# Weight conversion in PSUM banks, one exponential for two heads, and a 384 + 192 column split of the last attention product

## The chip, the cores and the metric

The kernel runs on one core of one Trainium2 chip. A core has five engines that run side by side, each through its own list of instructions in order: PE (matrix products, with a separate track PEld for loading weights), DVE (vector work), ACT (activation functions and copies), POOL (general work) and SP (which issues the transfers). The metric is device time in microseconds (us) of one execution; lower is better.

## The reference

Eight batches of eight heads go through linear attention with random features, and the result, 4608 tokens of width 512, goes through a two-layer network.

```python
def phi(x):
    proj = np.einsum('bhsd,md->bhsm', x, omega)        # 64 -> 128 features
    h = proj - np.sum(x * x, axis=-1, keepdims=True) / 2.0
    return np.exp(h - np.max(h, axis=-1, keepdims=True)) / np.sqrt(m)
kv = np.einsum('bhsm,bhsd->bhmd', k_p, v)
z = np.sum(k_p, axis=2)
num = np.einsum('bhsm,bhmd->bhsd', q_p, kv)
den = np.einsum('bhsm,bhm->bhs', q_p, z)[..., None] + 1e-06
x = num / den
...
h = x @ w_in                                            # 512 -> 2048
sp = np.maximum(h, 0.0) + np.log1p(np.exp(-np.abs(h)))
out = (h * erf(sp)) @ w_out                             # 2048 -> 512
```

The two weight matrices arrive as 64-bit floats; everything else is 32-bit.

## The kernel before

**Attention.** The work is cut into 32 pairs (batch, two heads), written `b_p` in the names. Sequence length is 576, so a pair has 1152 rows of q and k, the first head's 576 and then the second's. For each pair PE projects k and q into 128 features, three tiles of 384 rows each (`ppk`, `ppq`); DVE takes the maxima (`mxk`, `mxq`), ACT the exponentials (`fk`, `fq`); PE sums keys times values (`kvp`), which DVE or ACT copies to `kh` (with a rest `kl` from pair 8 on); PE turns the query features (`pt`, three tiles of 384), which DVE and ACT copy to `qh` (and a rest `ql`). The last product `nd` multiplies `kh` and `qh`: for each of the two heads it gives 64 rows of numerators and 64 rows of the denominator, repeated; the second head has them the other way up (`rows`). It is made in four tiles of 288 columns, one for each head and half. For the first eight pairs (`WHOLE = 8`) it is one product in 32-bit floats; from then on it is three products in fp32r, PE's faster 32-bit format, on a high part and a rest of each operand. For each tile ACT takes the logarithm of the denominators and then the exponential of its negative (`rc`, 64 rows each), and DVE multiplies numerators by it into `xs`.

**Network.** Each batch goes through two halves (`ph`) of 1024 hidden columns. The first layer gives tiles `h` (for the first three batches), later seven products `hS`, `hA` in place of eight; then softplus, erf and a product (`gs`, `hs`), a high part `gh` and a rest `gl`; the second layer gives tiles `o`. All these products have 288 columns and use three fp32r matmuls: high by high, high by rest, rest by high.

**Weights.** Each of 32 weight blocks is converted once, by `make`, the first time that it is needed (all in the first quarter of the run), and stored; later uses fetch the stored form. A 64-bit block `st` of 128 by 512 lands; `w_bias` scales its upper word into `wt`, `w_shift` shifts it, `w_sign` and `w_tail` (two DVE instructions with two inputs, `st` and `wt`) put in sign and tail, `w_high` rounds to fp32r and `w_rest` takes the difference. `wt` lies in ordinary on-chip memory (pool `gh`), bias and high may be done by POOL or ACT, the rest by DVE or POOL.

**Order.** Nothing is placed by hand. `build` lists all operations with their engines and costs, tiles and due times, and `Plan.order` goes through them as a list scheduler would: each engine, when free, takes the ready operation that is due first, if its tiles have a free slot. The order that comes out is fixed in the program. `SLOTS` gives slots in each pool (8 banks in PSUM, pool `ps`), `CAPS` how many of them one stream may hold at once: `att` attention tiles, `moe1` and `moe2` the network's, and `early(n)` replaces the cap of `att` for the four pairs of the first batch.

Of the kernel before, what the change touches and what calls it, by code (L numbers as in the profile page):

```python
# [319 lines left out]
def build(emit):  # L322
# [36 lines left out]
    def parts(t, src, keys):  # L359

        ks = range(2)
        pl.op("whigh", [("A", 0.63, -1e9), ("G", 0.7, WHG)], lambda e: E.w_high(e, t, src),
              reads=keys, writes=[(t, ("h", k)) for k in ks])
        pl.op("wrest", [("V", 0.68, -1e9), ("G", 1.3, 3.0)], lambda e: E.w_rest(e, t, src),
              reads=keys + [(t, ("h", k)) for k in ks], writes=[(t, ("l", k)) for k in ks])

    def make(u, t):

        nm = "_".join(str(c) for c in u)
        st = pl.tile("gl", f"st{nm}", [P, HW, 2], I32, "st")  # L370
# [12 lines left out]

    def unit(u, block=None):
# [127 lines left out]
    def attend(n, t0):  # L512
        a = pairs[n]
        x = xs[n] = pl.tile("xs", f"xs{a['nm']}", [P, 2, T])
        for j in range(2):
            for t in range(2):
                nd = pl.tile("ps", f"nd{a['nm']}_{j}_{t}", [P, 512], F32, "att", early(n))
                rc = pl.tile("rc", f"rc{a['nm']}_{j}_{t}", [P, T])
                c = range((j * S + t * T) // 384, (j * S + (t + 1) * T - 1) // 384 + 1)
                pl.op("nd", [("T", 0.5 if n < WHOLE else 3 * COST["mm"], -1e9)],  # L520
                      lambda e, j=j, t=t, nd=nd: E.attend(nd, a["kh"], a["kl"], a["qh"], a["ql"], j, t),
                      reads=[(a["kh"], 0), (a["kl"], 0)] + [(a["qh"], i) for i in c]
                      + [(a["ql"], i) for i in c], writes=[(nd, 0)],
                      plan=pair_time(n, t0 + 0.1 * j + 0.05 * t))
# [200 lines left out]
def tile_attention_moe(ctx: ExitStack, tc: tile.TileContext, qT, kT, vP, omT, w1, w2, out):  # L725
# [66 lines left out]
    class Emit:  # L792
# [243 lines left out]
```

## Time and profile before

| what | us |
|---|---|
| median of 3 runs | 1103.33 (1102.34 to 1104.43) |
| span of the profiled execution | 1101.4 |
| median less span | 1.9 |
| PE, DVE, ACT, POOL busy (shares) | 98%, 65%, 64%, 40% |
| transfers | 231 MB, 210 GB/s |

The profiled execution is known by its span, from the first to the last instruction of the program; the median of the runs is 1.9 us above it. Busy time of PE is the union of its matmuls, which overlap one another, so that a busy PE need not be at its peak: where times of single matmuls are needed, the distance from one start to the next is taken.

### The profile page before, as it was taken

Reading aid. Unit: us, or ns where it says so; the run is one execution under the profiler, and the core shown is the slowest. Engines: PE = TensorE matmul, PEld = TensorE weight load, DVE = VectorE, ACT = ScalarE, POOL = GpSimd, SP = SyncE. Lnnn points to the kernel's source line nnn. Section 1 sums busy time; section 2 is a strip of 40 time slices with the busy share of each in tenths; the row PEclk is TensorE's granted clock in tenths of the full one; section 3 lists DMA queues with packets and bytes.
Section 4 is the critical chain, followed back from the end, with each engine's and each line's share of the span. In section 5 each row is a group of like instructions: output and inputs, shape, how many; then the busy total and the mean of one; then the engine's idle time right before and its main releaser. Section 6 shows DMA issues by size and latency. Waiting matters only on the chain.

```text
span 1101.4 us, 21514 instructions
## 1 busy us (share of the span) xinstructions
PE 1074.1 (98%) x8272; PEld 1063.9 (97%) x8272; DVE 715.1 (65%) x1257; ACT 709.0 (64%) x1354; POOL 435.1 (40%) x353
## 2 busy tenths in 40 slices
PE   7798899999999999999999999999999999999998
PEld 6698899999999999999999999999999999999998
DVE  5967789876377575955757566675656766464541
ACT  7777769776578766756647667476566764654440
POOL 6535336210075294822436343343334413252300
PEclk9899899999999999999999999999999999999999
DMA  8546568675557666666666777657765666567771
GB/s 241 174 132 205 173 231 279 198 257 162 171 176 251 205 204 242 190 215 226 216 211 207 225 216 222 211 181 247 232 225 185 214 216 208 193 226 278 254 241 58
DMA packets 70117, 231.27 MB, mean 210 GB/s; under 512 B 8288, under 2 KB 8672, under 8 KB 70016
## 3 DMA queue, kind: packets, MB, share of 16 engines
q1 hardware_dynamic: 69952, 229.84, 63.9%
q8 instruction: 66, 1.08, 0.4%
q14 instruction: 35, 0.29, 0.1%
q0 software_dynamic: 64, 0.07, 0.0%
HBM read 195.26 MB, written 34.60 MB: 209 GB/s over the span
## 4 chain that ended last, share of the span: by engine, by line
PE 91%; DVE 4%; ACT 1%; issue 1%; DMA 1%; SPq 1%; POOL 0%; DVEq 0%
PE o L742 36%; PE h L742 13%; PE hS L742 11%; PE hA L742 8%; PE ppq L742 5%; PE kvp L742 5%; PE ppk L742 5%; PE nd L742 5%; PE pt L742 2%; DVE wt L742 1%; DMA uk<-kT 1%; SPq L742 1%; DVE qh L742 0%; DVE hs L742 0%; DVE mxk L742 0%
## 5 line engine op out<-in xcount | busy, mean ns | idle before, releaser
L742 PE MATMUL o<-gh,w 128*128 128x288 f32 x2048 | 444.8, 298 | 7.8 <-POOL w L742 7.4
L742 PEld LDWEIGHTS o<-gh,w 128*128 128x128 f32 x2048 | 338.9, 188 | 9.0 <-POOL w L742 8.0
L742 PE MATMUL o<-gl,w 128*128 128x288 f32 x1024 | 301.9, 295 | 0.0
L742 PEld LDWEIGHTS o<-gl,w 128*128 128x128 f32 x1024 | 192.7, 188 | 0.2
L742 PE MATMUL h<-xh,w 128*128 128x288 f32 x768 | 178.8, 305 | 0.9 <-ACT hs L742 0.9
L742 PE MATMUL hS<-xh,wS 128*128 128x288 f32 x640 | 165.7, 302 | 1.1 <-issue 1.1
L742 ACT ACTIVATE fk<-ppk,mxk 128x128 f32<-128x128 f32 x288 | 83.3, 371 | 78.0 <-DVE mxk L742 77.6
L742 PEld LDWEIGHTS h<-xh,w 128*128 128x128 f32 x768 | 131.2, 191 | 1.6 <-ACT hs L742 1.3
L742 PE MATMUL hA<-xh,w 128*128 128x288 f32 x480 | 122.1, 299 | 0.0
L742 ACT ACT_TABLE_LOAD x92 | 118.0, 1283 | 2.4 <-PEq L1027 0.7
L742 PEld LDWEIGHTS hS<-xh,wS 128*128 128x128 f32 x640 | 114.8, 189 | 1.3 <-issue 1.3
L742 PE MATMUL h<-xl,w 128*128 128x288 f32 x384 | 113.9, 297 | 0.0
L742 ACT ACTIVATE fq<-ppq,mxq 128x128 f32<-128x128 f32 x288 | 83.2, 371 | 40.0 <-DVE mxq L742 39.5
L742 POOL TENSOR_TENSOR gl<-hs,gh 128x576 fp32r<-128x576 f32 x50 | 86.5, 1753 | 42.2 <-ACT gh L742 25.8
L742 POOL TENSOR_TENSOR uq<-uq 64x576 f32<-64x576 f32 x40 | 46.4, 1178 | 139.6 <-DMA uq<-qT 98.1
L742 POOL TENSOR_TENSOR hs<-gs,hs 128x576 f32<-128x576 f32 x40 | 65.1, 1649 | 85.8 <-ACT gs L742 66.0
L742 DVE TENSOR_REDUCE mxk<-ppk 128x3 f32<-128x384 f32 x96 | 52.8, 556 | 68.9 <-PE ppk L742 67.8
L742 PE MATMUL hS<-xl,wS 128*128 128x288 f32 x320 | 94.5, 295 | 0.0
L742 POOL TENSOR_TENSOR uk<-uk 64x576 f32<-64x576 f32 x44 | 53.5, 1234 | 93.1 <-DMA uk<-kT 91.6
L742 ACT ACTIVATE gh<-hs 128x1152 fp32r<-128x1152 f32 x49 | 56.4, 1164 | 48.1 <-DVE hs L742 19.4
L742 PEld LDWEIGHTS hA<-xh,w 128*128 128x128 f32 x480 | 85.9, 189 | 0.0
L742 PE MATMUL ppk<-wk,uk 128*128 128x128 f32 x576 | 79.2, 279 | 4.4 <-DVE wk L742 4.1
(94 smaller groups left out, 2124.4 us busy)
## 6 DMA issues: line engine op xcount, KB each, us to landing
w<-wdw SPq DMA_DIRECT2D x184, 512.0 KB, 4.3
wS<-wdcS SPq DMA_DIRECT2D x80, 512.0 KB, 4.0
st<-w SPq DMA_DIRECT2D x32, 512.0 KB, 5.2
wdw<-w SPq DMA_DIRECT2D x32, 512.0 KB, 3.9
v<-vP SPq DMA_DIRECT2D x32, 325.0 KB, 3.5
w<-wdw SPq DMA_DIRECT2D x40, 256.0 KB, 3.7
out<-os SPq DMA_DIRECT2D x32, 288.0 KB, 4.0
uk<-kT SPq DMA_DIRECT2D x31, 288.0 KB, 4.2
```

The costliest lines, as they stand in the source:

```text
L742: return tc.keep_in_program_order(method(*args, **kwargs))
```

## The change

- `make` takes `wt` from the PSUM pool `ps` (one bank each, at most two at once, stream `wp`) and no longer from `gh`. POOL doesn't reach PSUM, so bias and high are on ACT alone, shift, sign, tail and rest on DVE alone, under new names (`pbias`, `pshift`, ...) and with new costs. The six instructions themselves stay the same.
- `attend` makes `nd` in tiles of 384 and 192 columns (`SPANS`). The two heads' logarithms of one span go into one `rc` tile of 128 rows, and one exponential covers both. There is one `rc` slot for each span.
- `early` gives the first four pairs up to seven banks, where it was five, and `att` may hold five, where it was four.

```diff
-CAPS = dict(st=2, wt=2, cv=2, att=4, moe1=3, moe2=2)
+CAPS = dict(st=2, wt=2, wp=2, cv=2, att=5, moe1=3, moe2=2)
...
+SPANS = ((0, 384), (384, 192))
...
-        w = pl.tile("gh", f"wt{nm}", [P, HW], I32, "wt")
-        pl.op("wbias", [("G", 0.8, WBG), ("A", 0.67, -1e9)], lambda e: E.w_bias(e, st, w),
+        w = pl.tile("ps", f"wt{nm}", [P, HW], I32, "wp")
+        pl.op("pbias", [("A", 0.67, -1e9)], lambda e: E.w_bias(e, st, w),
...
-        pl.op("wshift", [("V", 0.42, -1e9)], lambda e: E.w_shift(w), reads=[(w, 0)], writes=[(w, 0)])
+        pl.op("pshift", [("V", 0.68, -1e9)], lambda e: E.w_shift(w), reads=[(w, 0)], writes=[(w, 0)])
...
     def early(n):
-        return 5 if n < NP else None
+        return 7 if n < NP else None
...
-            act.activation(rc.ap[num], nd.ap[den, :T], AF.Ln, bias=eps[den])
+            act.activation(rc.ap[num], nd.ap[den, :w], AF.Ln, bias=eps[den])
...
-        def exp_den(self, rc, j):
-            num = rows(j)[0]
-            act.activation(rc.ap[num], rc.ap[num], AF.Exp, scale=-1.0)
+        def exp_den(self, rc):
+            act.activation(rc.ap, rc.ap, AF.Exp, scale=-1.0)
```

The new `attend`, which takes the place of the loop over heads and halves:

```python
for t, (c0, w) in enumerate(SPANS):
    rc = pl.tile(f"rc{t}", f"rc{a['nm']}_{t}", [P, w])
    nds = [pl.tile("ps", f"nd{a['nm']}_{j}_{t}", [P, 512], F32, "att", early(n)) for j in range(2)]
    for j, nd in enumerate(nds):
        pl.op("nd", [("T", (4 if n < WHOLE else 3) * COST["mm"] * w / T, -1e9)], ...)
    for j, nd in enumerate(nds):
        pl.op("ndlog", [("A", 0.25 + 0.00083 * w, -1e9)], ...)
    pl.op("ndexp", [("A", 0.2 + 0.00083 * w, -1e9)], lambda e, rc=rc: E.exp_den(rc), ...)
    for j, nd in enumerate(nds):
        pl.op("divide", [("V", 0.15 + 0.00105 * w, -1e9)], ...)
```

Because the planner sees other costs and slots, the whole order changes. Two places follow. The first is DVE's list in the second pair of the run, `0_1`, up to the two copies that make its `qh` (here `0_1` is the pair, a last number counts tiles, `wt1_0_1` is a weight block of the first layer). Before:

```order
L742 TENSOR_TENSOR w1_0_0_1_147<-wt1_0_0_254,w1_0_0_1_147 128x2x256
L742 TENSOR_REDUCE mxq_0_1_258<-ppq_0_1_2_286 128x3
L742 TENSOR_SCALAR wt1_0_1_269<-wt1_0_1_269 128x512
L742 SCALAR_TENSOR_TENSOR wt1_0_1_269<-st1_0_1_157,wt1_0_1_269 128x512
L742 TENSOR_REDUCE mxk_0_2_335<-ppk_0_2_0_322 128x3
L742 TENSOR_TENSOR xs_0_0_277<-nd_0_0_1_0_245,rc_0_0_1_0_290 64x288
L742 TENSOR_REDUCE mxk_0_2_335<-ppk_0_2_1_331 128x3
L742 TENSOR_REDUCE mxk_0_2_335<-ppk_0_2_2_338 128x3
L742 COPY qh_0_1_360<-pt_0_1_0_350 128x384
L742 TENSOR_TENSOR xs_0_0_277<-nd_0_0_1_1_247,rc_0_0_1_1_293 64x288
L742 SCALAR_TENSOR_TENSOR wt1_0_1_269<-st1_0_1_157,wt1_0_1_269 128x512
L742 COPY qh_0_1_360<-pt_0_1_2_367 128x384
```

Now, the same place up to the same two copies:

```order
L751 TENSOR_SCALAR wt1_0_0_264<-wt1_0_0_264 128x512
L751 SCALAR_TENSOR_TENSOR wt1_0_0_264<-st1_0_0_150,wt1_0_0_264 128x512 x2
L751 COPY kh_0_1_304<-kvp_0_1_278 128x2x64
L751 COPY kh_0_1_304<-kvp_0_1_278 128x128
L751 TENSOR_REDUCE mxk_0_2_314<-ppk_0_2_0_300 128x3
L751 TENSOR_REDUCE mxk_0_2_314<-ppk_0_2_1_310 128x3
L751 TENSOR_TENSOR xs_0_0_330<-nd_0_0_0_0_233,rc_0_0_0_298 64x384
L751 TENSOR_REDUCE mxk_0_2_314<-ppk_0_2_2_317 128x3
L751 TENSOR_TENSOR xs_0_0_330<-nd_0_0_1_0_240,rc_0_0_0_298 64x384
L751 COPY qh_0_1_345<-pt_0_1_0_333 128x384
L751 COPY qh_0_1_345<-pt_0_1_2_349 128x384
```

The second weight block (`wt1_0_1`) and the first block's rest have moved behind these copies, the copy of `kh` has come in from ACT, and the two copies of `qh` stand next to each other.

The second place is the conversion of `w2_0_0_0`, the block that the first second-layer product waits for. Before, POOL does its bias, high and rest, between those of other blocks:

```order
L742 TENSOR_SCALAR wt2_0_0_0_1250<-st2_0_0_0_1174 128x512
L742 TENSOR_TENSOR w1_1_3_12_1125<-wt1_1_3_1186,w1_1_3_12_1125 128x2x256
L742 TENSOR_SCALAR wt2_0_0_1_1268<-st2_0_0_1_1255 128x512
L742 TENSOR_SCALAR w2_0_0_0_13_1175<-wt2_0_0_0_1250 128x2x256
L742 TENSOR_TENSOR w2_0_0_0_13_1175<-wt2_0_0_0_1250,w2_0_0_0_13_1175 128x2x256
```

Now POOL has none of it, and DVE's list reads there:

```order
L751 TENSOR_SCALAR wt2_0_0_0_1320<-wt2_0_0_0_1320 128x512
L751 SCALAR_TENSOR_TENSOR wt2_0_0_0_1320<-st2_0_0_0_1206,wt2_0_0_0_1320 128x512
L751 TENSOR_REDUCE mxk_1_3_1375<-ppk_1_3_0_1331 128x3
L751 TENSOR_REDUCE mxk_1_3_1375<-ppk_1_3_1_1342 128x3
L751 TENSOR_REDUCE mxk_1_3_1375<-ppk_1_3_2_1347 128x3
L751 COPY qh_1_2_1370<-pt_1_2_1_1382 128x384
L751 TENSOR_TENSOR w1_1_3_12_1101<-wt1_1_3_1306,w1_1_3_12_1101 128x2x256
L751 SCALAR_TENSOR_TENSOR wt2_0_0_0_1320<-st2_0_0_0_1206,wt2_0_0_0_1320 128x512
L751 TENSOR_TENSOR xs_1_1_1297<-nd_1_1_1_1_1166,rc_1_1_1_1292 64x192
L751 COPY hs0_1_1_1340<-h010_1_1_1360 128x288
L751 TENSOR_SCALAR wt2_0_0_1_1425<-wt2_0_0_1_1425 128x512
L751 TENSOR_TENSOR w2_0_0_0_13_1207<-wt2_0_0_0_1320,w2_0_0_0_13_1207 128x2x256
```

On PE the first second-layer product moves from row 323 of the list to row 404: it stood in the middle of the products of `w1_1_1`, and now stands behind those of `w1_1_3` and most of pair `1_3`.

More of the change, by code (lines that the diff above doesn't have):

```diff
@@ L357, in store, with parts @@
               plan=clock[0] + 10.0, size=P * HW * 8)
-    def parts(t, src, keys):
+    def parts(t, src, keys, banked=False):
         ks = range(2)
-        pl.op("whigh", [("A", 0.63, -1e9), ("G", 0.7, WHG)], lambda e: E.w_high(e, t, src),
+        pl.op("phigh" if banked else "whigh", [("A", 0.63, -1e9)] + [("G", 0.7, WHG)] * (not banked),
+              lambda e: E.w_high(e, t, src),
               reads=keys, writes=[(t, ("h", k)) for k in ks])
-        pl.op("wrest", [("V", 0.68, -1e9), ("G", 1.3, 3.0)], lambda e: E.w_rest(e, t, src),
+        pl.op("prest" if banked else "wrest", [("V", 0.68, -1e9)] + [("G", 1.3, 3.0)] * (not banked),
+              lambda e: E.w_rest(e, t, src),
               reads=keys + [(t, ("h", k)) for k in ks], writes=[(t, ("l", k)) for k in ks])
@@ L514, in attend @@
         x = xs[n] = pl.tile("xs", f"xs{a['nm']}", [P, 2, T])
[L515 to L521, printed above, removed]
+        for t, (c0, w) in enumerate(SPANS):
+            rc = pl.tile(f"rc{t}", f"rc{a['nm']}_{t}", [P, w])
+            nds = [pl.tile("ps", f"nd{a['nm']}_{j}_{t}", [P, 512], F32, "att", early(n)) for j in range(2)]
+            for j, nd in enumerate(nds):
+                c = range((j * S + c0) // 384, (j * S + c0 + w - 1) // 384 + 1)
+                pl.op("nd", [("T", (4 if n < WHOLE else 3) * COST["mm"] * w / T, -1e9)],
+                      lambda e, j=j, c0=c0, w=w, nd=nd:
+                      E.attend(nd, a["kh"], a["kl"], a["qh"], a["ql"], j, c0, w),
@@ L529, in attend @@
-                pl.op("divide", [("V", 0.47, -1e9)], lambda e, j=j, t=t, nd=nd, rc=rc: E.divide(x, nd, rc, j, t),
-                      reads=[(nd, 0), (rc, 0)], writes=[(x, (j, t))])
+                      plan=pair_time(n, t0 + 0.1 * t + 0.05 * j))
+            for j, nd in enumerate(nds):
+                pl.op("ndlog", [("A", 0.25 + 0.00083 * w, -1e9)],
+                      lambda e, j=j, w=w, nd=nd, rc=rc: E.log_den(rc, nd, j, w),
+                      reads=[(nd, 0)], writes=[(rc, j)], set="exp")
@@ L532, in split @@
+            pl.op("ndexp", [("A", 0.2 + 0.00083 * w, -1e9)], lambda e, rc=rc: E.exp_den(rc),
+                  reads=[(rc, 0), (rc, 1)], writes=[(rc, 0), (rc, 1)], set="exp")
+            for j, nd in enumerate(nds):
+                pl.op("divide", [("V", 0.15 + 0.00105 * w, -1e9)],
+                      lambda e, j=j, c0=c0, w=w, nd=nd, rc=rc: E.divide(x, nd, rc, j, c0, w),
+                      reads=[(nd, 0), (rc, j)], writes=[(x, (j, i)) for i in range(t, 2)])
     def split(b, c):
@@ L904, in turn_rest, with attend, log_den, divide @@
             dve.tensor_sub(ql.ap[:, c], pt.ap[:, :3 * P], qh.ap[:, c].bitcast(F32))
-        def attend(self, nd, kh, kl, qh, ql, j, t):
-            c = slice(j * S + t * T, j * S + (t + 1) * T)
+        def attend(self, nd, kh, kl, qh, ql, j, c0, w):
+            c = slice(j * S + c0, j * S + c0 + w)
             if kh is kl:
-                pe.matmul(nd.ap[:, :T], lhsT=kh.ap[:, j, :], rhs=qh.ap[:, c], start=True, stop=True)
+                pe.matmul(nd.ap[:, :w], lhsT=kh.ap[:, j, :], rhs=qh.ap[:, c], start=True, stop=True)
                 return
             for i, (l, r) in enumerate(((kh, qh), (kh, ql), (kl, qh))):
-                pe.matmul(nd.ap[:, :T], lhsT=l.ap[:, j, :], rhs=r.ap[:, c], start=i == 0, stop=i == 2)
-        def log_den(self, rc, nd, j):
+                pe.matmul(nd.ap[:, :w], lhsT=l.ap[:, j, :], rhs=r.ap[:, c], start=i == 0, stop=i == 2)
+        def log_den(self, rc, nd, j, w):
             num, den = rows(j)
-            act.activation(rc.ap[num], nd.ap[den, :T], AF.Ln, bias=eps[den])
-        def exp_den(self, rc, j):
+            act.activation(rc.ap[num], nd.ap[den, :w], AF.Ln, bias=eps[den])
+        def exp_den(self, rc):
+            act.activation(rc.ap, rc.ap, AF.Exp, scale=-1.0)
+        def divide(self, x, nd, rc, j, c0, w):
             num = rows(j)[0]
-            act.activation(rc.ap[num], rc.ap[num], AF.Exp, scale=-1.0)
-        def divide(self, x, nd, rc, j, t):
-            num = rows(j)[0]
-            dve.tensor_mul(x.ap[num, t, :], nd.ap[num, :T], rc.ap[num])
+            dve.tensor_mul(x.ap.rearrange("p t c -> p (t c)")[num, c0:c0 + w], nd.ap[num, :w], rc.ap[num])
         def x_high(self, e, h, src, i, n):
```

11 lines of the change are left out of this document (3 added, 8 removed).

## Prediction

> **What bounds the kernel now.** I read the page first.
>
> ```profile
> span 1101.4 us, 21514 instructions
> PE 1074.1 (98%) x8272; PEld 1063.9 (97%) x8272; DVE 715.1 (65%) x1257; ACT 709.0 (64%) x1354; POOL 435.1 (40%) x353
> PE   7798899999999999999999999999999999999998
> PEclk9899899999999999999999999999999999999999
> ```
>
> PE is the bound, and it falls short only in the first six slices of 27.5 us. So a step is worth what it takes out of PE's gaps there, or adds to PE's own work anywhere. The windows view sizes the gaps (PE, PEld, DVE, ACT, POOL busy, then PE's granted clock):
>
> ```profile
> 14.50:58.80 44.30, 36.17 (x231) 30.25 (x229) 37.48 (x67) 34.75 (x102) 28.21 (x27) 0.88 0.61 193
> 27.00:35.00 8.00, 5.04 (x14) 3.33 (x14) 7.18 (x11) 4.69 (x14) 6.92 (x7) 0.57 0.33 127
> 35.00:58.80 23.80, 20.64 (x145) 18.28 (x144) 21.94 (x44) 19.03 (x56) 10.61 (x11) 0.93 0.49 167
> 106.00:116.00 10.00, 1.70 (x5) 0.79 (x4) 9.38 (x9) 9.93 (x13) 8.02 (x6) 0.68 0.50 184
> 116.00:140.00 24.00, 23.92 (x173) 23.92 (x174) 17.48 (x25) 17.96 (x32) 7.96 (x8) 0.92 0.50 168
> 116.00:220.00 104.00, 103.74 (x791) 102.67 (x792) 86.61 (x129) 80.97 (x167) 41.30 (x40) 0.98 0.67 220
> 460.00:536.00 76.00, 73.49 (x561) 72.51 (x560) 48.77 (x91) 45.16 (x89) 31.58 (x22) 0.98 0.65 213
> ```
>
> Where PE stalls, DVE is busy 90 to 94% (7.18 of 8.00, 21.94 of 23.80, 9.38 of 10.00): those stretches are DVE's. A stall also costs clock (0.57 and 0.68). The waits of PE, and the chain of work for PE's own pace:
>
> ```profile
> PE o L742 <- POOL w L742: 7.4, 2, 6.9
> PE nd L742 <- DVE qh L742: 6.8, 6, 2.5
> PE ppk L742 <- DVE xs L742: 0.4, 1, 0.4
> 38.58 2.06 PE ppk L742 x18
> 70.98 0.98 PE pt L742 x9
> 72.77 1.94 PE nd L742 x8
> 352.21 1.96 PE kvp L742 x18
> 1059.42 38.13 PE o L742 x288
> ```
>
> A plain 32-bit product is two records. So a projection of a pair (ppk, likewise ppq) takes 2.06 us, kvp 1.96, pt 0.98, a plain nd pair 1.94, and an fp32r matmul of 288 columns 38.13/288 = 132.4 ns.
>
> **Term A, the first four pairs (14.5 to 58.8).** PE has there nd of the first pair, three pairs of 2.06 + 2.06 + 1.96 + 0.98 + 1.94 = 9.0 us, and six fp32r matmuls: 1.9 + 27.0 + 0.8 = 29.7 of 44.3 us. Some 14 us are lost. DVE's timeline shows how (the last row is PE's, the first projection behind these pairs):
>
> ```profile
> 18.48 0.56 DVE L742 TENSOR_REDUCE mxq<-ppq 128x3 f32<-128x384 f32 x1 [3.04 <-PE ppq L742]
> 24.42 0.90 DVE L742 TENSOR_SCALAR wt<-wt 128x512 int32<-128x512 int32 x1
> 25.36 1.66 DVE L742 SCALAR_TENSOR_TENSOR wt<-st,wt 128x512 int32<-128x512 int32 x1
> 28.01 1.02 DVE L742 TENSOR_REDUCE mxk<-ppk 128x3 f32<-128x384 f32 x2
> 30.02 1.61 DVE L742 SCALAR_TENSOR_TENSOR wt<-st,wt 128x512 int32<-128x512 int32 x1
> 58.84 0.38 PE L742 MATMUL ppq<-wq,uq 128*128 128x128 f32 x2
> ```
>
> Work on a weight block that nobody needs yet (0.90 + 1.66, then 1.61) stands ahead of the copies of qh for which nd waits, and is stretched. The view of the tile wt says by what (minimum/median/maximum ns), with ACT's and DVE's rows on other tiles:
>
> ```profile
> L742 DVE SCALAR_TENSOR_TENSOR wt<-st,wt x64: 674/693/1801, 20.5 to 240.8; 128x512 int32<-128x512 int32 x64
> L742 DVE TENSOR_SCALAR wt<-wt x32: 410/422/1478, 20.0 to 239.7; 128x512 int32<-128x512 int32 x32
> L742 POOL TENSOR_SCALAR wt<-st x27: 641/665/1757, 19.3 to 237.0; 128x512 f32<-128x512 f32 x27
> L742 POOL TENSOR_SCALAR w<-wt x20: 617/618/1663, 31.8 to 241.7; 128x512 fp32r<-128x512 f32 x20
> L742 DVE TENSOR_TENSOR w<-wt,w x14: 674/683/1281, 23.4 to 242.3; 128x512 fp32r<-128x512 f32 x14
> L742 ACT ACTIVATE w<-wt x12: 613/631/633, 22.3 to 236.3; 128x512 fp32r<-128x512 f32 x12
> L742 ACT ACTIVATE rc<-nd,eps x128: 478/494/500, 18.7 to 957.2; 64x288 f32<-64x288 f32 x128
> L742 ACT ACTIVATE rc<-rc x128: 422/440/447, 20.4 to 957.7; 64x288 f32<-64x288 f32 x128
> L742 DVE TENSOR_TENSOR xs<-nd,rc x128: 436/452/463, 22.2 to 958.2; 64x288 f32<-64x288 f32 x128
> L742 DVE TENSOR_TENSOR ql<-pt,qh x72: 542/548/561, 195.4 to 947.4; 128x384 fp32r<-128x384 f32 x72
> L742 DVE TENSOR_TENSOR hs<-gs,hs x44: 1341/1350/2592, 91.0 to 1067.5; 128x1152 f32<-128x1152 f32 x44
> L742 DVE COPY hs<-h x29: 437/457/459, 66.0 to 440.9; 128x288 f32<-128x288 f32 x29
> ```
>
> DVE's conversion steps read two operands in ordinary memory and stretch to 1801 ns beside POOL; xs and ql, one operand in PSUM, never exceed their median by more than 3%. With wt in PSUM, I take the second behaviour. [...] The price of a step in PSUM isn't shown: from 452 at 288 columns and 548 at 384, 1.0 ns a column gives 676 at 512; the bounds are 422 (the shift now) and 1801, the step's worst. I take 680, the PSUM rows being the nearest.
>
> In the new order DVE does, from the first mxq of pair 0_1 to the last qh of pair 0_3: 18 maxima x 0.50 (1.02 for two), 11 conversion steps x 0.68, 6 qh x 0.52, 6 xs of 384 x 0.52 and 6 of 192 x 0.32 (the rows less 0.03 of overlap), and 2.8 of smaller copies: 27.4 us. ACT has as much there. At 92% (35:58.8) that is 29.8 us; from 18.48 it ends at 48.3, nd follows until 50.4, and the next ppq, at 58.84 now, could start 8.4 us earlier. ACT being as full, I take **7.0** (0 to 11).
>
> The extra banks by themselves: PE's only wait for one is 0.4 us. The single exponential adds no wait for PE: ACT's cost of a pair falls from 4 x (494 + 440) = 3.74 us to 2 x 576 + 2 x 412 + 522 + 358 = 2.86, by 0.85 ns a column (440 at 288, 631 at 512). Over 32 pairs 28 us leave ACT; from 220 us on PE is never short of it, so nothing of that counts.
>
> **Term B, up to the first second-layer product.** Before, its weight comes through POOL, and PE waits 6.9 us (waits, above): 8.3 of the ten us from 106 are lost, and 0.08 x 24 = 1.9 to the clock behind, 10.2 in all. Now the conversion is on ACT and DVE, and PE has 81 rows more ahead of it. What is late next is DVE: each conversion now costs it shift, two steps and rest, 4 x 0.68 = 2.7 us, with POOL's 18 rests among them and the stretching gone. From nd of pair 0_3 to the first use of w1_1_3 the new order gives PE 258 fp32r matmuls (34.2), 54 projections (12.0), kvp 6.0, pt 3.0, nd 6.4: 61.5 us. DVE has 39 conversion steps (26.5), 18 maxima (9.0), 16 copies of h (0.42 each, less the overlap: 6.7), 8 gates and rests of 1.35 (10.8), xs 4.7, the remainder 5.9: 63.6 us, more than PE. At 92% it takes 69.1, and PE loses 7.6. Gain 10.2 - 7.6 = **2.6** (-9 to +10). ACT, by the same count, has 58.8.
>
> **Term C, narrower products.** From pair 8 on, 24 pairs x 2 heads x 3 = 144 times two matmuls of 288 columns become one of 384 and one of 192. By columns 384 costs 132.4 x 4/3 = 176.5 and 192 costs 88: no change. But no fp32r matmul in this trace is narrower than 288. kvp has 65 columns and yet 1.96/18 = 109 ns a record, as pt with 128 columns has: there is a floor near 109. With it a pair of matmuls costs 176.5 + 109 - 264.8 = 20.7 ns more, 144 x 20.7 = **3.0 us** lost. The bounds are 0 and the plain price below. The plain pairs cost the same, floor or not.
>
> The Trainium skill ("TensorE: Matmul & The Clock Gate", section "LDWEIGHTS") speaks against this split: a load of 128 columns of weights takes 128/1.2, about 107 ns, whatever the matmul streams. By it the term would be (176.5 + 107 - 264.8) x 144 = 2.7 us, an estimate from that page, against 0 by columns; kvp's 109 agrees, though in plain 32 bits.
>
> **Sum.** Of the profiled 1101.4: - 7.0 - 2.6 + 3.0 = 1094.8; the median lies 1.9 higher: **1096.7 us**. The 2.5 us of PE gaps in 460:536 and the rest I leave.
>
> **Rivals.**
> 1. *The narrow fp32r product runs at the plain rate* (slower). Plain nd of 288 takes 1.94/4 = 485 ns, 323 at 192. Then a pair of matmuls costs 176.5 + 323 - 264.8 = 235 ns more, 33.8 us in place of 3.0: 1127.5. It decides as soon as the rate drops at all below some width under 288. For it: no row at that width; against: kvp's floor looks like a fixed load, not a rate. Chance 0.15.
> 2. *DVE doesn't hold 92%* (slower). At 83% (86.61 of 104.00, 116:220) A takes 33.0 in place of 29.8 and B 76.6 in place of 69.1, 10.7 more: 1107.4. Gain and loss meet at 86%, where 91.0 us of DVE take 6.6 more. For it: POOL, 40% busy, loses its share while DVE and ACT gain. Chance 0.15.
> 3. *Nothing changes*: DVE at 85 to 88%, 1101 to 1105.5. Chance 0.12.
> 4. *Stalls go altogether*: A 11, B 8, 460:536 2.5 with 3.0 lost: 1084.8. Chance 0.13.
>
> My forecast (1089 to 1101) has 0.45. Faster by over 0.2% (about what a measurement of this kernel can tell from no change) is 0.45 + 0.13 = 0.58, within it 0.12, slower 0.30. The range of 8 in 10, 1085 to 1114, takes in rivals 2 and 3 and reaches to 4; it leaves out 1 and the lower half of 4.
>
> **What would show it.** A: the ppq behind nd of pair 0_3 starts near 51 to 52 us, no DVE step on wt is over 0.75 us. B: no PE wait for POOL w; DVE at 90% or more between 52 and 120 us, with PE waits on DVE w or qh of 5 to 10 us in all. C: nd rows of 192 some 109 ns apart; at 88 or at 160 and over, C is wrong. If the first 140 us gain 10 us and the total doesn't, C or the later order took it.

## The result, and the profile after

The change made the kernel slower: 1107.07 us median (1106.46 to 1116.03) against 1103.18 before, ratio 1.0053 (95% interval 1.0027 to 1.0079). The forecast was 1096.7 us (1089 to 1101) and faster. The profiled execution has a span of 1109.5 us; its own time, 1111.45, lies 4.4 us over the median, and one cause of that is visible below.

The page of the changed kernel, its head and PE's two rows over 40 slices of 27.7 us:

```profile
span 1109.5 us, 21441 instructions
PE 1077.9 (97%) x8272; PEld 1066.6 (96%) x8272; DVE 725.4 (65%) x1291; ACT 698.6 (63%) x1312; POOL 394.7 (36%) x309
PE   7899999999999999899999999999999899999998
PEclk9999999999999999999999999999999999999999
```

Before, PE's row fell short only in the first six slices. Now there are two new eights, in the 17th slice (444 to 472 us) and in the 32nd (860 to 888 us), where no weights are converted and no caps of the first pairs apply. The windows view (PE, PEld, DVE, ACT, POOL busy, then PE's granted clock) sizes them; the last row is of the kernel before, where the second stretch has no gap:

```profile
14.50:58.80 44.30, 36.92 (x245) 32.43 (x244) 32.13 (x64) 36.65 (x101) 14.63 (x15) 0.92 0.58 162
106.00:116.00 10.00, 6.28 (x50) 5.82 (x48) 9.86 (x14) 9.81 (x19) 0.00 (x0) 1.00 0.08 32
116.00:220.00 104.00, 101.04 (x774) 98.85 (x774) 86.73 (x146) 80.59 (x161) 19.69 (x19) 1.00 0.73 248
460.00:536.00 76.00, 72.14 (x547) 71.37 (x546) 48.58 (x89) 42.72 (x78) 28.45 (x18) 0.98 0.68 218
840.00:920.00 80.00, 77.17 (x591) 76.69 (x590) 51.94 (x93) 49.52 (x87) 29.29 (x22) 0.98 0.61 195
840.00:920.00 80.00, 80.00 (x628) 80.00 (x627) 51.57 (x97) 52.15 (x90) 34.69 (x25) 1.00 0.65 204
```

The hole at 106 to 116 us is smaller (PE 6.28 of 10.00, it was 1.70) and costs no clock (1.00, it was 0.68). The two stretches at the end lose 3.9 and 2.8 us of PE and 2% of the clock. In the first of them the kernel before had gaps too, 2.5 us in short waits, and the same 0.98; in the second it had none. PE's waits (waited for; us in total, times, longest):

```profile
PE nd L751 <- DVE ql L751: 4.7, 4, 2.8
...
PE ppq L751 <- ACT fq L751: 3.7, 2, 2.1
PE hS L751 <- DVE u L751: 3.6, 1, 3.6
PE ppq L751 <- DVE xs L751: 3.0, 2, 1.8
PE kvp L751 <- ACT fq L751: 1.8, 1, 1.8
...
PE ppq L751 <- DVE w L751: 0.9, 1, 0.9
...
PE nd L751 <- DVE qh L751: 0.2, 1, 0.2
```

The two waits that bounded the first stages are gone: o for POOL's w (7.4 us before) and nd for DVE's qh (6.8, now 0.2). In their place stand waits for a free bank: ppq reads neither fq, xs nor w, so a ppq that waits for one of them waits for the reader of the tile that holds its bank. They add up to 7.6 us. The longest wait of the first row (2.8 us) and the wait of hS for u are the two late stalls. The timeline around the earlier one, in order of time (DVE's, POOL's and PE's rows):

```profile
460.85 6.80 DVE L751 TENSOR_TENSOR gl<-hs,gh 128x1152 fp32r<-128x1152 f32 x3
461.55 4.89 POOL L751 TENSOR_TENSOR gl<-hs,gh 128x576 fp32r<-128x576 f32 x2
464.69 0.29 PE L751 MATMUL hA<-xh,w 128*128 128x288 f32 x1
467.57 0.55 DVE L751 TENSOR_REDUCE mxq<-ppq 128x3 f32<-128x384 f32 x1
468.04 0.44 DVE L751 TENSOR_TENSOR u<-hS,hs 128x288 f32<-128x288 f32 x1
468.54 0.61 PE L751 MATMUL hS<-xh,wS 128*128 128x288 f32 x1 [3.55 <-DVE u L751]
```

Three rests gl stand in a row in DVE's list, ahead of the sum u that sets free the bank of the next first-layer product hS. They take 1.83, 2.57 and 2.55 us, the second wholly and the others in part beside POOL's two rests; the median of DVE's 38 rests gl is 1.36. PE stands still for 3.6 us. The other one:

```profile
859.08 3.29 POOL L751 TENSOR_TENSOR gl<-hs,gh 128x576 fp32r<-128x576 f32 x2 [1.28 <-ACT gh L751]
860.37 1.43 PE L751 MATMUL pt<-ident,fq 128*128 128x128 f32 x9
861.50 2.08 DVE L751 TENSOR_TENSOR gl<-hs,gh 128x1152 fp32r<-128x1152 f32 x1
863.50 0.55 DVE L751 TENSOR_REDUCE mxk<-ppk 128x3 f32<-128x384 f32 x1
863.97 1.47 DVE L751 TENSOR_TENSOR ql<-pt,qh 128x384 fp32r<-128x384 f32 x3
864.57 0.69 PE L751 MATMUL nd<-qh,kh 128*128 128x384 f32 x1 [2.77 <-DVE ql L751]
```

PE has turned the query features (pt) by 861.8, and the three ql that nd waits for stand behind a stretched gl.

Two sizes of the prediction can be read off at once. DVE's conversion steps, now on a bank (minimum/median/maximum ns), are never over 0.70 us, where they reached 1.80 before:

```profile
L751 DVE SCALAR_TENSOR_TENSOR wt<-st,wt x64: 680/695/697, 23.1 to 239.5; 128x512 int32<-128x512 int32 x64
L751 DVE TENSOR_SCALAR wt<-wt x32: 680/692/700, 22.4 to 237.5; 128x512 int32<-128x512 int32 x32
```

And the narrow product, three matmuls of 384 columns and then four of 192, by their starts:

```profile
505.51 0.34 PE L751 MATMUL nd<-qh,kh 128*128 128x384 f32 x1
505.69 0.34 PE L751 MATMUL nd<-ql,kh 128*128 128x384 f32 x1
505.87 0.34 PE L751 MATMUL nd<-qh,kl 128*128 128x384 f32 x1
506.04 0.25 PE L751 MATMUL nd<-qh,kh 128*128 128x192 f32 x1
506.13 0.27 PE L751 MATMUL nd<-ql,kh 128*128 128x192 f32 x1
506.24 0.28 PE L751 MATMUL nd<-qh,kl 128*128 128x192 f32 x1
506.35 0.27 PE L751 MATMUL nd<-qh,kh 128*128 128x192 f32 x1
```

384 columns take 0.53/3 = 177 ns, 192 take 0.31/3 = 103 on the mean (90 behind a matmul of 384, then 110 and 110); over all fp32r ones the medians are 175.5 and 111.5. By them a pair costs 175.5 + 111.5 - 264.8 = 22 ns more than two of 288, times 144: 3.2 us. Taken three at a time, with the shorter first one, it is less: the medians of a group are 525.5 and 313.5 ns, against 396.5 for 288 columns before, and 48 groups of each make 2.2 us.

### The profile page after: what moved, and what is told of

It is laid out like the page before. It is cut to its first block, busy times and chain, and to the rows that moved or that the text cites. A ratio compares the mean times of both kernels' runs of the same rounds, so it can differ in the third digit from the quotient of the medians.

```text
span 1109.5 us, 21441 instructions
## 1 busy us (share of the span) xinstructions
PE 1077.9 (97%) x8272; PEld 1066.6 (96%) x8272; DVE 725.4 (65%) x1291; ACT 698.6 (63%) x1312; POOL 394.7 (36%) x309
## 4 chain that ended last, share of the span: by engine, by line
PE 90%; DVE 4%; DMA 2%; ACT 2%; issue 1%; SPq 0%; ACTq 0%; DVEq 0%
PE o L751 36%; PE h L751 13%; PE hS L751 11%; PE hA L751 8%; PE ppq L751 5%; PE kvp L751 5%; PE ppk L751 5%; PE nd L751 4%; PE pt L751 2%; DMA st<-w 1%; DVE gl L751 1%; DVE gh L751 1%; DVE mxk L751 0%; DMA v<-vP 0%; ACT L751 0%
## 5 line engine op out<-in xcount | busy, mean ns | idle before, releaser
L751 PE MATMUL h<-xh,w 128*128 128x288 f32 x768 | 174.3, 302 | 0.7 <-issue 0.7
L751 PE MATMUL hS<-xh,wS 128*128 128x288 f32 x640 | 161.0, 301 | 3.6 <-DVE u L751 3.6
L751 POOL TENSOR_TENSOR uq<-uq 64x576 f32<-64x576 f32 x52 | 59.4, 1161 | 234.8 <-DMA uq<-qT 162.8
L751 PEld LDWEIGHTS h<-xh,w 128*128 128x128 f32 x768 | 128.7, 188 | 1.4 <-issue 0.9
L751 POOL TENSOR_TENSOR uk<-uk 64x576 f32<-64x576 f32 x48 | 56.8, 1202 | 141.7 <-DMA uk<-kT 129.2
L751 POOL TENSOR_TENSOR hs<-gs,hs 128x576 f32<-128x576 f32 x44 | 69.5, 1602 | 100.3 <-ACT gs L751 63.4
L751 POOL TENSOR_TENSOR gl<-hs,gh 128x576 fp32r<-128x576 f32 x52 | 92.1, 1797 | 36.2 <-ACT gh L751 27.2
L751 ACT ACTIVATE rc<-nd,eps 64x384 f32<-64x384 f32 (+1 forms) x128 | 63.4, 496 | 36.4 <-PE nd L751 33.9
L751 PE MATMUL ppq<-wq,uq 128*128 128x128 f32 x576 | 77.4, 276 | 7.8 <-ACT fq L751 3.7
```

Of the source, the lines that this page charges most:

```text
L751: return tc.keep_in_program_order(method(*args, **kwargs))
```

## The experiments

Two theories stood at the start. **Late waits:** the first stages gained about what was forecast, the narrow product took 3.2 us of it, and the two stalls at 461 and 861 us, which the new order made and the prediction left out, took the rest. **Banks:** two of eight banks for weights make PE wait in the first 180 us, and the gain of the first stages never came. Runs whose name begins with x keep the changed kernel's list of instructions, so that one thing differs; those with e let the scheduler make a new list from one part of the change or without one. All are timed in interleaved rounds with the kernel before (medians 1102.69 to 1103.42), in four sets, each on a chip of its own. Differences between two of them are taken from their ratios, times 1103 us.

The last column is from each trace: the time from the start of the 385th second-layer product (265 to 277 us) to the end. In every order the same PE rows stand ahead of it, 1892 of 8272 (only e7 has 28 fewer), and no weight is converted behind it. So it separates the late stretch from the first 270 us, which scatter: four traces that have the same list up to there (first profile, a0, x6, x5) reach it at 271.0, 265.8, 267.6 and 274.1 us, the kernel before at 274.0. The late stretch repeats: 838.5 us in the first profile, 838.6 in a0.

| run | median us | ratio to before (95%) | median clock | late, us |
|---|---|---|---|---|
| before | 1103 | 1 | 0.991 | 827.4 |
| a0, the changed kernel again | 1107.82 | 1.0048 (1.0033 to 1.0064) | 0.9945 | 838.6 |
| x1, 288 and 288 columns | 1104.52 | 1.0020 (1.0005 to 1.0035) | 0.995 | 834.7 |
| x2a, weights in ordinary memory, same banks | 1114.85 | 1.0110 (1.0093 to 1.0127) | 0.992 | 839.3 |
| x2b, the same, banks given out anew | 1108.15 | 1.0049 (1.0034 to 1.0063) | 0.993 | 838.8 |
| x4, x1 with three rests moved | 1098.77 | 0.9963 (0.9949 to 0.9977) | 0.997 | 829.1 |
| x5, changed kernel, three rests moved | 1099.73 | 0.9979 (0.9964 to 0.9995) | 0.9975 | 831.5 |
| x6, changed kernel, one rest moved | 1104.90 | 1.0016 (1.0006 to 1.0025) | 0.996 | 835.3 |
| x7, x5 with two exponentials | 1108.11 | 1.0045 (1.0029 to 1.0062) | 0.9935 | 831.8 |
| e1, changed kernel without the conversion | 1114.52 | 1.0098 (1.0083 to 1.0112) | 0.9895 | 838.1 |
| e2, before with the conversion | 1097.87 | 0.9954 (0.9939 to 0.9969) | 0.9945 | 826.1 |
| e3, before with one exponential, 288 | 1101.84 | 0.9984 (0.9975 to 0.9993) | 0.992 | 827.8 |
| e3b, the same, 384 and 192 | 1105.86 | 1.0025 (1.0015 to 1.0036) | 0.990 | 830.8 |
| e5, before with more banks | 1099.59 | 0.9967 (0.9955 to 0.9979) | 0.997 | 827.6 |
| e6, changed kernel with 288 and 288 | 1101.41 | 0.9986 (0.9975 to 0.9998) | 0.9955 | 831.1 |
| e7, before, conversion and one exponential | 1103.50 | 1.0002 (0.9994 to 1.0011) | 0.992 | 830.9 |
| e8, before, conversion and more banks | 1102.41 | 1.0001 (0.9988 to 1.0013) | 0.996 | 827.3 |

### The changed kernel again (a0_after_again)

No edit.

> The changed kernel once more, as the yardstick for the runs beside it. Its profiled run above was 1111.45 us, 4.4 us over its median of 1107.07, and lost 4.7 us against the kernel before around 860 to 905 us of the span (PE waited 2.9 us there for DVE's ql). If that stall belongs to the order, it comes back in a run near 1107 us. If it belongs to that one execution, the span is near 1105 us and the stall is missing.

It comes to 1107.82, and both late stalls are back (3.5 and 2.8 us), at a span of 1104.4. So they belong to the order. What doesn't come back is the loss of the first profile's early stage:

```profile
14.50:58.80 44.30, 38.93 (x292) 34.76 (x291) 37.05 (x75) 40.03 (x113) 18.01 (x18) 1.00 0.64 187
```

The granted clock is 1.00 here, where the first profile had 0.92 in the same window. The first projection behind the first four pairs starts at 53.0 us, against 58.1 in the first profile and 58.8 before. This run, the fastest of its six, is the better one to read the terms from, but it shows the early gain at its best. Against the profile of before, the 385th second-layer product starts 8.2 us earlier (265.8 against 274.0), the 865th 7.9 earlier, the 961st 5.5, the 2017th 3.3; the 2209th is 1.7 us later and the last 2.4. The gain is there by 270 us, and it goes between 440 and 910 us.

### Even columns in the same order (x1_even_columns)

```diff
         def attend(self, nd, kh, kl, qh, ql, j, c0, w):
+            c0, w = (0, T) if c0 == 0 else (T, T)
```

so that 0 and 384 become 0 and 288; likewise in `log_den` and `divide`.

> The changed kernel's order kept instruction for instruction; only the last product is made in 288 and 288 columns in place of 384 and 192. Theory 'narrow product': a 192-column fp32r matmul cost 111.5 ns in the trace and a 384-column one 175.5, so 22 ns x 144 = 3.2 us come back: about 1103.9 us (3.2 less than the changed kernel beside it, 2.5 to 4). Rival 'the order': columns cost nothing in sum, the later waits do; then less than 1 us comes back. Nothing before pair 8 (about 190 us) should move by more than 0.5 us.

1.0048 - 1.0020 is 3.1 us, as the theory of the narrow product had it. By the late column it is 3.9. Everything else of the loss stays: both late stalls are in its trace (3.7 us at 458, 2.8 at 854).

### Weights back in ordinary memory, with and without their banks (x2a_weights_sbuf_same_banks, x2b_weights_sbuf_freed_banks)

```diff
+    for t in plan.streams["wp"]:
+        t.pool = "gh"
+    replace("gh", 6)      # slots given out anew in order of time, the longest free first
+    replace("ps", 8)      # x2b only: the same for the eight banks
```

> The changed kernel's order kept; wt lies in ordinary memory again, and the banks that it held stay as they are given out, so that every other tile keeps its bank. Theory 'conversion price': DVE's two-input steps on wt stretch beside POOL again, their mean goes from 693 ns to 750 to 880 ns (6 to 18 us more DVE work over 64 steps and 32 rests; the shift falls from 692 to about 420, 8.7 us less), and the time changes by -2 to +4 us. Rival 'banks': by itself this run says nothing of them except that ppq's 0.9 us for a bank held by a weight block goes.

> As the run before, but the eight banks are given out anew among the other tiles, in the same order of instructions, the longest free one first. Theory 'banks' (two of eight banks for weights make PE wait): PE's waits of ppq and kvp for DVE xs, ACT fq and DVE w, 9.4 us in the changed kernel, fall below 3 us, and the time is 4 to 8 us less than with the banks unchanged. Rival 'ACT is late' (PE waits for a bank only because ACT's exponentials are behind, and then would wait for their results): the waits change their names, and the time differs by less than 1.5 us.

x2a loses 1.0110 - 1.0048 = 6.8 us, more than the 4 expected. Its two-input steps stretch again, up to 1637 ns, and their mean is 829 ns, as expected; since the shift gets shorter, DVE's whole conversion work grows by only 4 us, so that it probably counts where the long ones fall. All of the loss lies ahead of the 385th second-layer product (273.3 us, late column as in a0), and none of it in the first four pairs: the first projection behind them comes at 52.3 us, a0's at 53.0. x2b gains 1.0110 - 1.0049 = 6.7 us on x2a. The waits of x2a, then those of x2b:

```profile
PE ppq L751 <- DVE xs L751: 5.4, 5, 1.7
...
PE ppq L751 <- ACT fq L751: 3.0, 2, 2.7
```

```profile
PE ppq L751 <- ACT fq L751: 2.7, 1, 2.7
...
PE ppq L751 <- DVE xs L751: 1.3, 2, 0.7
```

The waits of ppq for banks fall from 8.4 to 4.0 us, not below the 3 expected. So both have a price, of one size: weights on banks are worth 6.8 us in this order, and giving their two banks to the others is worth 6.7. Neither is quite alone in its run: in x2a ACT's conversion steps take 2 us more in all (41.8 against 39.7), and the weights share the six slots of `gh` again; in x2b all eight banks are given out by another rule, which was not tried with the weights left on them. x2b ends where the changed kernel does. The theory of banks is right about a price, and not about the result: the price was covered by what it bought.

### Three rests moved (x4_rests_moved), one rest moved (x6_one_rest_moved), three moved with 384 and 192 columns (x5_rests_moved_384_192)

```diff
+    move(find("rest", "gl5_1_3"), find("turnrest", "ql_7_0", 2))
+    move(find("rest", "gl2_1_3"), find("divide", "xs_4_0", 3))
+    move(find("rest", "gl2_1_2"), find("hadd", "hs3_0_0", 4))
```

`move(a, b)` puts one operation of the finished list behind another. The second-layer products that read these gl come some 80 to 100 PE rows later, so the rests can wait. x4 is x1 with all three, x5 the changed kernel with all three, x6 the changed kernel with the first alone.

> As x1_even_columns (the changed order, 288 and 288 columns), with three of DVE's instructions moved in its list: the rests gl of batch 2, second half, blocks 2 and 3, behind the sums and quotients that stood after them, and the rest gl of batch 5, second half, block 3, behind the three rests ql of pair 7_0. Theory 'late waits': PE's waits hS <- DVE u near 459 us (3.7 us) and nd <- DVE ql near 856 us (2.8 us) shrink below 1 us each, and with the clock that they cost 5 to 6 us go: about 1099 us (1097.5 to 1101), under the kernel before. Rival 'DVE is full there': the work is only late elsewhere, new waits of 3 us and more come within 15 us, and the time stays within 1.5 us of 1104.5.

> The changed kernel exactly, with only the rest gl of batch 5 moved behind the rests ql of pair 7_0; the two others stay. The wait near 856 us (2.9) shrinks below 1 us, the one near 459 us (3.6) stays. Theory 'waits add up, each with the clock that it costs': 1103 to 1105 us, about half of the way from 1107.8 to the 1099.7 of three moved. Rival 'the first wait is made up later by slack': 1100 to 1101.5, all of the gain by the last wait alone.

> The changed kernel exactly, with its 384 and 192 columns, and only the three rests gl moved in DVE's list as in x4_rests_moved. Theory 'the two add up' (late waits 5.7 us, narrow product 3.3 us, each by itself): 1107.8 - 5.7 = 1102.1 us (1100.5 to 1103.5), 3.3 above x4_rests_moved and within 2 us of the kernel before. Rival 'the narrow product makes the waits': with 384 and 192 columns the waits come back elsewhere, and it stays above 1105.

x4 gains 6.3 us on x1 and ends at 1098.77: the late waits are shown, and DVE is not full there. x6 takes 3.5 us of the changed kernel's loss away and x5 another 4.1, so the two waits add up. The late column, which the scatter of the first 270 us doesn't reach, says the same: 838.6, then 835.3, then 831.5 us. x5, the change as it was made with three instructions in other places, is faster than the kernel before (0.9979); it was expected at 1102.1 and came to 1099.7, since the narrow product shows only 1.8 us between x4 and x5 (2.4 by the late column), within the scatter of the runs. Two of x5's twelve runs took 1107 us at a clock of 0.990, the other ten 1099.0 to 1102.3 at 0.996 to 0.999; its trace is of one of the two, and what it lost lies in the first 190 us. The windows of x6 and then of x5, around the two stalls:

```profile
460.00:536.00 76.00, 72.13 (x551) 71.36 (x550) 47.55 (x91) 41.99 (x78) 25.14 (x17) 0.98 0.67 217
840.00:920.00 80.00, 79.05 (x613) 78.41 (x612) 52.78 (x95) 49.80 (x86) 31.34 (x22) 1.00 0.61 201
```

```profile
460.00:536.00 76.00, 75.14 (x578) 74.23 (x579) 49.79 (x94) 45.97 (x88) 31.45 (x20) 1.00 0.72 231
840.00:920.00 80.00, 79.05 (x614) 78.41 (x613) 53.46 (x95) 49.75 (x85) 31.34 (x23) 1.00 0.64 205
```

Where a rest is moved, PE gets its time back and the clock its 0.02. 0.02 x 76 is 1.5 us: the first wait costs 3.0 us of PE (75.14 less 72.13) and 1.5 of clock, together 4.5, and the other one 1.9 (79.05 less 77.17) and 1.6, together 3.5. The runs say 4.1 (5.2 by medians) for the first and 3.5 (2.9) for the other. The clock is not always lost: in x1's trace the same second stall leaves it at 1.00.

### Two exponentials again (x7_two_exponentials)

```diff
-            act.activation(rc.ap, rc.ap, AF.Exp, scale=-1.0)
+            for j in range(2):
+                num = rows(j)[0]
+                act.activation(rc.ap[num], rc.ap[num], AF.Exp, scale=-1.0)
```

> The order of x5_rests_moved_384_192 (the changed kernel with three rests moved), with an exponential for each head again, two instructions of 64 rows in place of one of 128: ACT gets 64 instructions and 28 us more. Theory 'ACT isn't what PE waits for': within 1.5 us of 1099.7. Rival 'ACT is late in the first 180 us' (PE's waits for banks on ACT fq, 3 us, and on DVE xs, 3 us, grow, since six more exponentials stand in each of the first pairs' lists): 1102 to 1105, with the first projection behind the first four pairs 1 us and more later.

It loses 1.0045 - 0.9979 = 7.3 us, more than either theory gave. PE's waits of x5 and of x7:

```profile
PE ppq L751 <- ACT fq L751: 2.8, 2, 2.1
```

```profile
PE ppq L751 <- ACT fq L751: 4.0, 3, 2.1
...
PE hS L751 <- ACT fq L751: 1.0, 1, 1.0
```

New waits on ACT make some 2 us of it. The median clock of its runs is 0.004 lower, 4.4 us; that the waits cause this is likely by what the other runs show, but it wasn't tried apart, and at one clock, 0.997, x7's run of 1105.1 us still lies 5 above x5's three of 1099.2 to 1100.4. So the split stays open. The late column is the same as x5's (831.8 and 831.5 us), so the loss lies in the first 270 us. There the rival put it, but the mark that it named is missing: the first projection behind the first four pairs is not later (56.5 against 56.6). So the exponential that the prediction priced at nothing carries much of the change; that ACT needs the room, with conversions on it, fits, and is not shown further.

### The changed kernel without the conversion, and the conversion alone (e1_weights_as_before, e2_psum_conversion_alone)

The edit of `make` and `parts` in the diff, undone in the changed kernel (e1) and made alone in the kernel before (e2).

> The changed kernel with the weight conversion as before (ordinary memory, POOL allowed), planned anew; one exponential, 384 and 192 columns and the more banks stay. Theory 'price and banks cancel' (conversion in PSUM saved 7 us in the changed order and its two banks cost 7): this comes out within 3 us of the changed kernel, 1104 to 1110, with PE waits on POOL w or DVE qh back and those on ppq <- DVE xs, ACT fq gone. Rival 'PSUM conversion is the gain of the first 60 us': the first projection behind the first four pairs falls back from 53.0 to 57 us or later, and the time is 4 us or more above the changed kernel. Rival 'PSUM conversion is the loss': under 1103 us.

> The kernel before with the weight conversion in PSUM alone, planned anew: per-head exponentials, 288 columns, attention caps of four and five as before. Theory 'price and banks cancel': no stretched steps, but six banks for the rest: PE's waits for banks (ppq, ppk or kvp for DVE xs or ACT fq) of 5 us and more in the first 240 us, and a time within 4 us of the kernel before, 1099 to 1107. Rival 'PSUM conversion is a clear gain': 1090 to 1098. What it loses behind 240 us, if anything, is the replanned order's, since no weight is converted there.

e2 gains 5.1 us, more than the theory that price and banks cancel allows: with the list made for it, the conversion on banks wins. e1 loses 5.5 us against the changed kernel; the rival on the gain of the first 60 us had the sign right, but its first projection comes at 56.2 us and it waits later (3.0 us at 109, 2.9 at 140). And e1 has the same late stalls (2.6 us at 472, 2.8 at 868), though no weight lies in a bank: they don't come from the conversion.

### One exponential alone, with even and with narrow columns (e3_one_exponential_alone, e3b_one_exponential_384_192)

The new `attend` alone in the kernel before, with `SPANS = ((0, 288), (288, 288))` and with the change's own.

> The kernel before with one exponential for both heads alone, 288 and 288 columns, planned anew. ACT loses 64 instructions of 440 ns, 28 us. Theory 'ACT isn't what PE waits for': within 2 us of the kernel before by that, and whatever more it shows comes as single waits of PE on DVE (ql, u, qh) of 1 to 4 us that the new order put there. Rival 'held banks': the two logarithms ahead of one exponential hold two banks longer, PE waits for banks (ppq, pt or nd <- DVE xs) by 3 us or more in all, 1105 to 1110.

> The kernel before with one exponential and 384 and 192 columns alone, planned anew (weights and caps as before). The even columns planned the same way gave 1101.8. Theory 'narrow product': 3.2 us more, about 1105 (1103.5 to 1106.5). In DVE's list no long rest stands straight ahead of the three ql of pair 7_0 and no row of three rests ahead of the sum u near 460 us, so no PE wait on DVE ql or u of 2.5 us and more behind 220 us. Rival 'the late waits come with the narrow product': such waits, and 1108 and more.

e3 gains 1.8 us, e3b loses 2.8; the narrow product costs 4.5 between the two (3.0 by the late column), with another order in each. e3b has no wait over 1.5 us behind 220 us. So the late stalls don't come with the narrow product alone either.

### More banks alone, and pairs of parts (e5_banks_alone, e6_even_columns_replanned, e7_psum_and_one_exponential, e8_conversion_and_banks)

e5: the line `CAPS` with `att=5` and the 7 in `early` alone. e6: the changed kernel with `SPANS` even. e7: e2 with the attend of e3. e8: e2 with the caps of e5.

> The kernel before with only the two caps raised (five to seven banks for the first four pairs, four to five for the others), planned anew. The prediction had it that banks alone are worth nothing, as PE's only wait for one was 0.4 us: 1101 to 1105.5, and what differs comes from single waits of PE on DVE or ACT. Rival 'banks matter even before': the first projection behind the first four pairs 2 us and more ahead of 58.8 us, and 1098 to 1101.

> The changed kernel with 288 and 288 columns, planned anew (conversion in PSUM, one exponential, more banks). In DVE's list the three rests gl of batch 2, second half, still stand ahead of the sum u, so the wait hS <- DVE u of 3 to 4 us near 457 us should be there; the rest gl of batch 5 no longer stands ahead of ql of pair 7_0, so the wait near 856 us should be missing. Theory 'the late waits are where the list puts long rests ahead of what PE needs': 1104.5 - 3 = 1101.5 us (1099 to 1104). Rival 'the late waits go with the conversion in PSUM or the banks whatever the list': a wait of 2.5 us and more at 840 to 870 us again, and 1104 and more.

> The kernel before with the conversion in PSUM and one exponential at 288 and 288 columns; caps of four and five banks as before, planned anew. If the two parts' gains add up (5.5 and 1.6 us of the two alone) it is 1096.3 us. But in DVE's list the rest gl of the second half's block 3 stands ahead of two rests ql in batches 4, 5 (about 695 and 855 us); if POOL works on another rest gl at the same time, PE waits 1.5 to 3 us on ql at each, and it comes to 1099 to 1102.

> The kernel before with the conversion in PSUM and the raised caps, 288 columns and per-head exponentials, planned anew. Alone they gave 5.5 and 3.5 us. If the gains add up, 1094 us; if both remove the same waits of the first 130 us, 1096 to 1098. In DVE's list one rest gl of batch 2 stands between rests ql of pair 4_0 near 460 us: a wait of 1 to 1.5 us there, none of 2.5 us and more behind 200 us.

Banks alone gain 3.6 us, and the first projection behind the four pairs comes at 53.2 us, about where a0 has it: the prediction's "nothing" was wrong. With the conversion alone (e2) it comes at 57.1. The parts don't add up: of the conversion (5.1), the exponential (1.8) and the banks (3.6), e7 keeps 0, e8 keeps 0 and e6, with all three, 1.5. Each new list has its own stalls. e6 has the wait on u in the place that was read off its list (3.8 us) and none at 860. e7 missed its forecast, and for another reason than the one given: not ql, but

```profile
PE h L751 <- DVE w L751: 8.5, 2, 5.8
```

at 104 to 117 us, a weight's rest late on DVE. e8 has ACT full in the first four pairs (42.33 of 44.30 us) and then

```profile
PE h L744 <- ACT hs L744: 5.0, 2, 4.5
```

which fits x7: conversion without the single exponential leaves ACT behind.

## Why the prediction was wrong, point by point

- **What bounds the kernel**: right for the first 140 us, and incomplete. "PE is the bound, and it falls short only in the first six slices" was true of before; that the change could make new stalls elsewhere was not asked. And "those stretches are DVE's" misreads the third of its rows: at 106 to 116 us ACT is fuller (9.93 of 10.00, DVE 9.38), and what PE waits for there is POOL's w.
- **Term A, 7.0 us**: the size was right by luck. a0 shows 5.8 us (53.0 against 58.8); the other traces of the same list show 4.0 (x6), 2.3 (x5) and 0.7 (the first profile, with a clock of 0.92). On the prediction's own stretch, from the first mxq of pair 0_1 to the last qh of pair 0_3, DVE's work was sized right, 26.8 us for 27.4, but it doesn't hold 92%: it is busy 26.8 of 31.2 us (86%; before, 34.0 of 36.7) and ACT 28.2 (90%), and PE waits for banks. And unstretched steps are not what brings the gain: with the weights back in ordinary memory it stays (x2a, 52.3 us), and "the extra banks by themselves", taken as nothing, give 5.6 us of it (e5) and 3.6 of the whole time. That two banks for weights cost some 6.7 us (x2b against x2a) the sum didn't have. The steps' price of 0.68 us was right (0.69). The reason given for their stretching, two operands in ordinary memory, is not all of it: the shift reads one there, and by the prediction's own row it too went from 422 to 1478 ns.
- **"Nothing of that counts"**, on the single exponential: wrong. Undone in the same order it costs 7.3 us (x7), in the first 270 us, which the sentence left out; "from 220 us on PE is never short of it" holds but for a wait of 1.0 us.
- **Term B, 2.6 us**: right in size in a0, and not by its working. a0 is 5.8 us ahead at the end of A and 8.2 at 266 us, 2.4 more. PE's wait for POOL's w is gone, as said, and DVE is 89% busy from 52 to 120 us (60.49 of 68.00), but the waits on DVE w or qh of 5 to 10 us didn't come (0.9 and 0.2); ppq for banks took their place.
- **Term C, 3.0 us**: right, 2.2 to 3.2 by the pace of the rows, 3.1 between a0 and x1, 2.4 to 3.9 by the late column. The floor of 103 to 112 ns at 192 columns agrees with the 107 ns that the Trainium skill ("TensorE: Matmul & The Clock Gate", section "LDWEIGHTS") gives for a load of 128 columns of weights. PEld's records of these loads are longer, 186 ns at the least, and overlap.
- **The step that failed** is the end of the sum: "The 2.5 us of PE gaps in 460:536 and the rest I leave." The whole order changed, and the rest was priced at zero. Three rests in DVE's list behind 440 us cost 7.6 us (x5 against a0; 7.1 by the late column). With that, - 5.8 - 2.4 + 3.2 + 7.6 is + 2.6 us, where a0's trace is 3.0 longer than that of before (1104.4 less 1101.4): 8.2 us gained up to the 385th second-layer product and 11.2 lost behind it. By medians a0 is 5.1 us over before (1107.82 less 1102.69); since the late stretch repeats, the 2 us between lie in the first part, where the runs scatter and a0's trace is the best of four.
- **Rivals**: the second one, DVE at 83%, gave 1107.4, the measured time to 0.3 us, by luck and by a mechanism that isn't there: DVE holds 86 to 89%, and the first stages did gain. The first (the narrow product at the plain rate) is excluded by 111.5 ns against 323. The last line of what would show it, "if the first 140 us gain 10 us and the total doesn't, C or the later order took it", is what happened, with 8.2 us by 266 us, and with both.

Why the scheduler puts these rests there was not settled. They appear in the changed kernel and without the conversion (both), with even columns (one of the two), and in none of the single parts (e2, e3, e3b, e5) or of the two pairs (e7, e8). What the lists that have them share is the single exponential together with the raised caps; no run has these two alone. The list is made with a rest at 1.36 us, and in the stalls it takes 1.83 to 2.57.

## What to carry to other kernels

Where an edit makes a scheduler write a new list, the list itself is a part of the change: read it on the busiest partner of the bound engine for long instructions that stand straight ahead of what the bound engine waits for, over the whole run, and price them stretched. A term for "the rest stays as it was" needs a range of its own; here it was as large as the gain. And before dropping such a change, look whether a few instructions put elsewhere give the gain back: three of 21441 instructions turned + 0.5% into - 0.2%, and - 0.4% without the narrow product (x4), next to the conversion alone (e2, 1097.87 us).

## What the runs showed of the hardware

**A short lack of work costs PE more than the lack.** The windows of the first profile of the changed kernel, two us each (columns as above: PE, PEld, DVE, ACT, POOL, then granted clock), and one of a0:

```profile
20.00:22.00 2.00, 1.54 (x14) 1.35 (x13) 1.54 (x3) 1.08 (x2) 1.49 (x2) 1.00 1.05 218
22.00:24.00 2.00, 0.69 (x6) 0.70 (x7) 1.69 (x4) 1.98 (x8) 0.00 (x0) 1.00 1.03 239
24.00:26.00 2.00, 2.00 (x14) 2.00 (x13) 0.54 (x1) 1.95 (x6) 0.52 (x1) 0.63 1.00 247
26.00:28.00 2.00, 2.00 (x11) 2.00 (x11) 0.74 (x3) 0.94 (x2) 1.97 (x3) 0.50 0.69 162
28.00:30.00 2.00, 2.00 (x11) 1.98 (x10) 1.28 (x3) 1.26 (x5) 2.00 (x2) 0.50 0.36 133
30.00:32.00 2.00, 2.00 (x11) 1.45 (x9) 1.67 (x4) 0.91 (x4) 1.92 (x3) 0.66 0.01 3
...
30.00:32.00 2.00, 0.86 (x7) 0.86 (x8) 1.91 (x4) 1.81 (x7) 0.00 (x0) 1.00 0.00 0
```

From 22 to 24 us PE is idle for 1.3 of 2 us, and then, though busy again, runs at half clock for some 7 us: (0.37 + 0.50 + 0.50 + 0.34) x 2 = 3.4 us lost, 0.003 of the span. In a0 (last row) a window with PE busy 0.86 of 2.00 us cost no clock. Between 10 and 1095 us the eighteen traces show 50 such falls to 0.50, of 3.41 us (34 times), 6.83 (12) or 10.24 (4), so each costs 1.7, 3.4 or 5.1 us of PE's pace, as far as PE is the bound there; in the 3.41 us ahead of them PE had been busy for 0.0 to 2.0. So the same program has runs with one such loss more or less, and they show as steps: x4's seven runs are 1101.4 and 1102.4 us at a clock of 0.994, 1098.0 to 1099.2 at 0.997 and 1096.2 at 1.000. The Trainium skill ("TensorE: Matmul & The Clock Gate", section "What's actually happening") describes a monitor with free-running windows of 3413 ns that halves the clock after an idle one; that it hits or misses the same gap fits these runs, and the lengths are one, two and three such windows, though here PE wasn't idle for a whole one (busy 2.23 of the 4 us from 20 to 24). For a comparison at 0.2% this means many runs, and a look at the clock of each.

**Where an operand lies decides who stretches.** DVE's two-input steps on a PSUM bank kept 0.68 to 0.70 us whatever POOL did. The rests gl, two operands in ordinary memory, took 1.34 to 1.36 us in the first profile where POOL stood still and 1.41 to 2.57 where it worked all through them. The shift, one operand in ordinary memory, stretched as well, to 1.48 us before. The bank is not free, though: by x2b against x2a, two of eight cost as much as the weights on banks gain.
